# Local attention in units of two heads over 512 tokens, with the first expert products taken chunk by chunk between the units

## The chip, the cores and the metric

The kernel runs on one core of a Trainium2 chip. The engines named here are PE (TensorE, matrix products and transposes), ACT (ScalarE), DVE (VectorE), POOL (GpSimd) and SP (SyncE, whose queue issues the loads and stores). The metric is the device time of one launch in microseconds (us). The kernel before takes 873.11 us, the median of 3 runs (872.82 to 873.40).

## What is computed

Three steps follow each other, in float32 data with float64 weights for the two expert layers:

```python
# attention: 4 batches, 8 heads, 512 local and 32 global queries, head size 64
mask = np.abs(pos[:, None] - pos[None, :]) <= 32
s_l = concat([scale * q_l @ k_g.T, where(mask, scale * q_l @ k_l.T, -1e9)])
out_l = softmax(s_l) @ concat([v_g, v_l])
out_g = softmax(scale * q_g @ k_all.T) @ v_all
x = concat([out_g, out_l], axis=2)            # 2304 tokens x 512
# first expert layer: 512 -> 2048 -> 512
h = x @ w_in
y = elu(h) @ w_out
# second expert layer: 512 -> 1536 -> 512
xn = y / rms(y) * rms_g
out = (silu(xn @ w_gate) * (xn @ w_val)) @ w_o2
```

## The kernel before, in words

**Blocks.** The 2048 local tokens are four blocks of 512 (a batch each). A block needs its attention output `x` (four tiles of 128 tokens), its transpose `xT` (four chunks `c` of 128 features, each as a high and a low half in a reduced float type, since every large product is done in the three passes of `PASSES`, line 29), and then for each of 16 slices `j` of the hidden layer an *h product* (`mm1`, L127: 12 matmuls, three for each chunk) and a *y product* (`mm2`, L151: 12 matmuls, summed over all `j` in four PSUM tiles). Between them stands the activation (`act1` with `elu_a`, L137 and L120): on ACT a relu and an exp, on DVE a maximum, on ACT the high half of `g`, on DVE its low half.

**Attention units.** There are 16 local units `u`, four for each block. Each has five steps: S (`a_S`, 64 small matmuls), E (`a_E`: eight masked maxima on DVE, each followed by an exp on ACT), T (`a_T`: eight transposes on PE and two copies ET on ACT), PV (`a_PV`, 64 small matmuls) and N (`a_N`: the division, on DVE). S takes the load `kq`, PV the load `v`. Before the change, unit `u` is one tile of 128 tokens with all eight heads, so that each chunk of `xT` needs all four units of its block. Units 0 to 3 form the front; units 4 to 7 run inside block 0 for block 1, and so on.

**Weights.** They come as float64 words and are turned into two float32 halves, a pair of 128x512 tiles at a time: `abs` on ACT (L86), a shift (L93) and an or (L94) on DVE, the high half on ACT (`hi`, L97), the low half on DVE (`lo`, L100). Block 0 needs 16 such pairs, numbered 0 to 15 in `order1`: of each four, two are for `w_in` and feed four h products, and two are for `w_out` and feed two y products each. Pairs 0 to 2 are turned in the front, the others during block 0 (`w1_decode`, L394).

**Order.** PE always follows the written order. In the front (the `with` that starts behind L415) ACT and DVE follow it too; inside the blocks the builder's scheduler orders them, held by `issue_after`. Block 0 runs through `moe_block` (L324): for each `j` an h product, then the y product of `j - 1`, with the unit's steps between by `att_slot` (L299). The last lines of the block transpose `x` of the next block (`a_X`, L286) and subtract the low halves. The queue on SP is a single row: a load whose buffer is still in use holds all loads behind it.

**Idle products.** At the start PE does `NIDLE` = 61 matmuls of 64x64 zeros (L358) while the first load is on its way.

Of the kernel before, what the change touches and what calls it, by code (L numbers as in the profile page):

```python
# [21 lines left out]
P = 128  # L22
# [7 lines left out]
NIDLE = 61  # L30
# [11 lines left out]
def fused_kernel(ctx: ExitStack, tc: tile.TileContext, kq, vl, gkq, gv, w_in, w_out, w_gate, w_val, w_o2, rms_g, consts, out):  # L42
# [47 lines left out]

    def dec_bits(x, raw):
        word = words(raw)
        nc.vector.tensor_scalar(out=i32(x), in0=i32(x), scalar1=3, scalar2=None, op0=ALU.logical_shift_left)  # L93
        nc.vector.scalar_tensor_tensor(out=i32(x), in0=word[:, :, 0], scalar=29, in1=i32(x), op0=ALU.logical_shift_right, op1=ALU.bitwise_or)  # L94
# [32 lines left out]
    def mm1(xT, j, n):  # L127
        h = hps.tile([P, 512], F32, tag="h", name="h")
        G, o = j // 4, (j % 4) * P
        k = 0  # L130
        for c in range(4):
            for ws, xs in PASSES:
                nc.tensor.matmul(h[:, :n], W1[c, G][:, ws, o:o + P], xT[c][:, xs, :n], start=(k == 0), stop=(k == 11))  # L133
                k += 1
        return h

    def act1(h, n, fn=None):  # L137
# [4 lines left out]
        return g  # L142

# [51 lines left out]
    with ExitStack() as ls:  # L195
# [5 lines left out]
        zero = ac.tile([P, 64], BF16, name="zero")  # L201
# [15 lines left out]
        def load_v(u):  # L217
            if u < 16:
# [4 lines left out]
                t = t[:, :2080].rearrange("p (i h d) -> p i h d", i=4, h=8)  # L223
                nc.sync.dma_start(out=t, in_=vl[u].rearrange("p (i h d) -> p i h d", i=4, h=8))
                v_t[u] = t

        def a_S(u, pools):
            T = u % 4
            m = 0 if T == 0 else (2 if T == 3 else 1)
            t = kq_t.pop(u)  # L230
            ss = [pools[i][0].tile([P, 4, P], F32, tag=pools[i][1], name="s") for i in range(2)]
            for pr in range(4):
                for i in range(4):
                    for par in range(2):
                        r = slice(64 * par, 64 * par + 64)
                        nc.tensor.matmul(ss[par][32 * i:32 * i + 32, pr, :], t[r, pr, 224 + 32 * i:256 + 32 * i], t[r, pr, 32 * i:32 * i + 128],  # L236
                                         start=True, stop=True)
            s_t[u] = ss

        def a_E(u):  # L240
# [3 lines left out]
            T = u % 4  # L244
            mk_u = mask32[:, 0 if T == 0 else (2 if T == 3 else 1), :]
            for par in range(2):
                for pr in range(4):
                    nc.vector.tensor_tensor_reduce(out=e[par][:, pr, :], in0=ss[par][:, pr, :], in1=mk_u, scale=-SCALE, scalar=3.0e38,  # L248
                                                   op0=ALU.add, op1=ALU.min, accum_out=mx[:, par, pr:pr + 1])
                    nc.scalar.activation(e[par][:, pr, :], e[par][:, pr, :], AF.Exp, bias=mx[:, par, pr:pr + 1], scale=-1.0)  # L250
            e_t[u] = e

        def a_T(u, par, pool, tag):
            pt = pool.tile([P, 512], F32, tag=tag, name="ptp")
            for pr in range(4):
                nc.tensor.transpose(pt[:, pr * P:(pr + 1) * P], e_t[u][par][:, pr, :], ident)  # L256
# [16 lines left out]
        def a_N(u):  # L273
            b, T = u // 4, u % 4
            if T == 0:
                x_t[b] = moe.tile([P, 4, 512], F32, tag="x32", name="x")
            x = x_t[b][:, T, :].rearrange("p (a e d) -> p e a d", a=4, e=2)
# [1025 lines left out]
```

## Time and profile before

| | us |
|---|---|
| median of 3 runs | 873.11 |
| the profiled execution, its own time | 874.14 |
| its span, first to last instruction | 872.2 |
| PE busy in the span | 853.0 (98%) |
| DVE busy | 572.8 (66%) |
| ACT busy | 462.5 (53%) |

The trace counts microseconds from the start of the span. A row of the timeline gives the start, the length, the engine, the line, the operation with its tiles, the count, and in brackets the idle time before it and what ended that. "PEclk" is the clock that was granted to PE as a share of 2.4 GHz: 0.5 is the lower level, 1.2 GHz.

### The profile page before, as it was taken

To read this page: it belongs to the slowest core of one execution; us is meant where nothing else is said; L and a number is where in the kernel's file an instruction comes from. 1 tells how busy PE (TensorE), PEld (TensorE's weight loads), DVE (VectorE), ACT (ScalarE), POOL (GpSimd) and SP (SyncE) were. 2 spreads that over 40 slices of the span, in tenths; PEclk is the share of its full clock that TensorE was granted. 3 is DMA by queue.
4 is the path that set the end of the run, shared out by engine and by line. 5 is a ranking of instruction groups with operands and counts; after the bars stand their busy time and mean duration, and the time that the engine had idled before them with its cause. 6 is when DMAs were issued, how large, how long until landed. Compare 5 with 4: busy or idle time off the path is not lost.

```text
span 872.2 us, 16347 instructions
## 1 busy us (share of the span) xinstructions
PE 853.0 (98%) x6703; PEld 713.8 (82%) x6703; DVE 572.8 (66%) x1119; ACT 462.5 (53%) x788; POOL 8.0 (1%) x10
## 2 busy tenths in 40 slices
PE   7789999999999999999999999999999999999998
PEld 5567788888888888777878888878999888888998
DVE  3899637656575565544378788897987655555663
ACT  4789545555564455433273677764555444443442
POOL 0000000000000000000030000000000000000000
PEclk8899999999999999999999999999999999999999
DMA  9896525765578766442500687879523232329102
GB/s 355 327 381 232 196 84 204 260 240 204 210 280 281 235 211 218 163 168 94 171 26 25 219 292 240 260 246 340 248 75 119 73 97 73 98 72 397 62 25 86
DMA packets 92126, 165.49 MB, mean 190 GB/s; under 512 B 4884, under 2 KB 59284, under 8 KB 86932
## 3 DMA queue, kind: packets, MB, share of 16 engines
q1 hardware_dynamic: 92052, 164.45, 54.1%
q8 instruction: 53, 0.87, 0.4%
q14 instruction: 21, 0.17, 0.1%
HBM read 128.26 MB, written 36.18 MB: 189 GB/s over the span
## 4 chain that ended last, share of the span: by engine, by line
PE 88%; DVE 4%; DMA 3%; ACT 3%; issue 1%; SPq 0%; DVEq 0%; ACTq 0%
PE y L154 19%; PE h L133 18%; PE A L799 14%; PE c L1148 14%; PE Q L799 11%; PE pg L813 2%; DMA kq<-in_kq 2%; PE s L236 1%; PE yg L729 1%; PE hg L713 1%; PE o L269 1%; PE ptp L256 1%; PE og L833 1%; DVE dx L94 1%; DVE wA L100 1%
## 5 line engine op out<-in xcount | busy, mean ns | idle before, releaser
L154 PE MATMUL y<-g,wA 128*128 128x512 f32 x768 | 198.0, 401 | 4.4 <-DVE g L141 3.7
L133 PE MATMUL h<-xT,wA 128*128 128x512 f32 x768 | 186.6, 392 | 1.0 <-DVE xT L294 1.0
L154 PEld LDWEIGHTS y<-g,wA 128*128 128x128 f32 x768 | 140.5, 189 | 40.2 <-issue 5.7
L133 PEld LDWEIGHTS h<-xT,wA 128*128 128x128 f32 x768 | 143.7, 188 | 32.0 <-DVE xT L294 1.2
L799 PE MATMUL A<-xc,wS 128*128 128x512 f32 x576 | 138.9, 392 | 0.1
L799 PEld LDWEIGHTS A<-xc,wS 128*128 128x128 f32 x576 | 107.1, 188 | 23.1 <-DVE pp L852 0.8
L1148 PE MATMUL c<-wH,p 128*128 128x256 f32 x1008 | 125.3, 284 | 0.0
L1148 PEld LDWEIGHTS c<-wH,p 128*128 128x128 f32 x1008 | 123.0, 192 | 0.2
L799 PE MATMUL Q<-xc,wS 128*128 128x512 f32 x432 | 104.4, 391 | 0.7 <-DVE t L843 0.7
L799 PEld LDWEIGHTS Q<-xc,wS 128*128 128x128 f32 x432 | 80.2, 188 | 17.5 <-DVE t L843 1.2
L843 DVE TENSOR_TENSOR t<-t,Q 128x512 f32<-128x512 f32 x72 | 48.9, 684 | 49.2 <-ACT t L846 34.1
L838 ACT CAST p<-pp 128x512 fp32r<-128x512 f32 x84 | 51.3, 620 | 55.7 <-PE c L1148 51.1
L122 ACT ACTIVATE e<-h 128x512 f32<-128x512 f32 x48 | 28.8, 601 | 95.0 <-PE h L133 94.9
L846 ACT COPY t<-A 128x512 f32<-128x512 f32 x72 | 41.9, 585 | 62.3 <-PE A L799 62.1
L839 DVE TENSOR_TENSOR p<-pp,p 128x512 fp32r<-128x512 f32 x84 | 56.7, 686 | 21.6 <-ACT p L838 21.6
L124 DVE SCALAR_TENSOR_TENSOR e<-e,h 128x512 f32<-128x512 f32 x48 | 32.8, 683 | 54.6 <-ACT e L123 54.4
L604 DVE TENSOR_TENSOR wS<-wraw,wS 128x1024 fp32r<-128x1024 f32 x42 | 51.2, 1218 | 14.8 <-ACT wS L603 13.2
L140 ACT CAST g<-e 128x512 fp32r<-128x512 f32 x64 | 39.7, 620 | 35.6 <-DVE e L124 22.1
L141 DVE TENSOR_TENSOR g<-e,g 128x512 fp32r<-128x512 f32 x64 | 44.1, 689 | 19.2 <-ACT g L140 18.7
L603 ACT CAST wS<-wraw 128x1024 fp32r<-128x1024 f32 x42 | 43.9, 1045 | 1.7 <-DMA wraw<-wS 1.7
L250 ACT ACTIVATE E<-E,mx 128x128 f32<-128x128 f32 x128 | 39.7, 390 | 8.5 <-DVE mx L248 8.5
L849 ACT ACTIVATE t<-t 128x512 f32<-128x512 f32 x36 | 22.8, 632 | 39.0 <-DVE t L843 39.0
(197 smaller groups left out, 907.6 us busy)
## 6 DMA issues: line engine op xcount, KB each, us to landing
wH<-wH SPq DMA_DIRECT2D x20, 1024.0 KB, 9.2
wraw<-wS SPq DMA_DIRECT2D x36, 512.0 KB, 4.1
raw<-in_moe_w_out SPq DMA_DIRECT2D x14, 1024.0 KB, 5.6
raw<-in_moe_w_in SPq DMA_DIRECT2D x8, 1024.0 KB, 8.0
raw<-in_moe_w_gate SPq DMA_DIRECT2D x6, 1024.0 KB, 6.8
raw<-in_moe_w_val SPq DMA_DIRECT2D x6, 1024.0 KB, 5.5
wS<-raw SPq DMA_DIRECT2D x24, 256.0 KB, 2.2
gvr<-in_gv SPq DMA_DIRECT2D x8, 640.0 KB, 4.4
```

The costliest lines, as they stand in the source:

```text
L133: nc.tensor.matmul(h[:, :n], W1[c, G][:, ws, o:o + P], xT[c][:, xs, :n], start=(k == 0), stop=(k == 11))
L140: hi = nc.scalar.copy(g[:, 0, :n], e[:, :n])
L141: mark[:] = hi, nc.vector.tensor_tensor(out=g[:, 1, :n], in0=e[:, :n], in1=f(g[:, 0, :n]), op=ALU.subtract)
L154: nc.tensor.matmul(ys[dc][:, :n], W2[j][:, ws, dc * P:(dc + 1) * P], g[:, gs, :n], start=(j == 0 and k == 0), stop=(j == 15 and k == 2))
L603: nc.scalar.copy(t[:, :, 0, :], raw)
L604: nc.vector.tensor_tensor(out=t[:, :, 1, :], in0=raw, in1=f(t[:, :, 0, :]), op=ALU.subtract)
L799: nc.tensor.matmul(ps, w[:, 2 * (q % 4) + c, ws, :], x[:, c, xs, :], start=(first and c == 0 and z == 0), stop=(c == 1 and z == 2), skip_g ...
L838: hi = nc.scalar.copy(p[:, 0, :], src)
L839: mark[:] = hi, nc.vector.tensor_tensor(out=p[:, 1, :], in0=src, in1=f(p[:, 0, :]), op=ALU.subtract)
L843: mark[1] = nc.vector.tensor_tensor(out=t, in0=t, in1=ps, op=ALU.add)
L846: mark[0] = nc.scalar.copy(t, ps)
L1148: nc.tensor.matmul(ch[t // 2][:, 256 * (t % 2):256 * (t % 2) + 256], p[:, pl, t * P:(t + 1) * P], w[:, wl, :], start=(n in (0, 1, 3) and i ...
```

## The change

**Units.** Unit `u` of a block is now a pair of heads (one chunk `c` = u mod 4 of the features) over all 512 tokens of the block. The loads `kq` and `v` are laid out anew by the host for that; the counts and shapes of the matmuls, masks, exps and transposes of a unit stay as they were.

**Front.** Since unit `c` fills chunk `c` of `x` for the whole block, it can be transposed at once (`x_turn`, `x_hi`, `x_lo`), and the three matmuls of that chunk can be done for the h products of j = 0 and j = 1 (`mm1` with a range of chunks) before the next unit is done.

**Block 0.** Its first part (j = 0 to 3) is written out with ACT and DVE in written order; the rest is a loop of four `j` at a time in which each y product stands one h product later than before, and pairs are turned behind the marks of the activation before.

**Loads and idle products.** The first weight pair is loaded ahead of unit 0's `v`, the second ahead of unit 1's `v`, and the loads of unit 4 and of pairs 4 and 5 are written ahead of the front. `NIDLE` is 155, with matmuls of 32x32 on four column groups in turn.

```diff
-NIDLE = 61
+NIDLE = 155
-    def mm1(xT, j, n):
-        h = hps.tile([P, 512], F32, tag="h", name="h")
+    def mm1(xT, j, n, h=None, cs=range(4)):
+        if h is None:
+            h = hps.tile([P, 512], F32, tag="h", name="h")
...
-        for c in range(4):
-            for ws, xs in PASSES:
-                nc.tensor.matmul(h[:, :n], W1[c, G][:, ws, o:o + P], xT[c][:, xs, :n], start=(k == 0), stop=(k == 11))
-                k += 1
+        for c in cs:
+            for k, (ws, xs) in enumerate(PASSES):
+                nc.tensor.matmul(h[:, :n], W1[c, G][:, ws, o:o + P], xT[c][:, xs, :n], start=(c == 0 and k == 0), stop=(c == 3 and k == 2))
...
-            x = x_t[b][:, T, :].rearrange("p (a e d) -> p e a d", a=4, e=2)
+            x = x_t[b][:, :, c * P:(c + 1) * P].rearrange("p t (e d) -> p e t d", e=2)
...
+        def x_turn(b, c, pool, tag):
+            pt = pool.tile([P, 512], F32, tag=tag, name="xtp")
+            for T in range(4):
+                nc.tensor.transpose(pt[:, T * P:(T + 1) * P], x_t[b][:, T, c * P:(c + 1) * P], ident)
+            return pt
...
-            nc.tensor.matmul(idle[:64, :64], zero, zero, start=True, stop=True)
+        for k in range(NIDLE):
+            g = 32 * (k % 4)
+            nc.tensor.matmul(idle[g:g + 32, :32], zero, zero, start=True, stop=True)
...
+        w1_load()
         load_v(0)
         load_kq(1)
         w1_load()
         load_v(1)
         load_kq(2)
-        w1_load()
         load_v(2)
...
             a_S(0, ATT2)
             a_E(0)
...
+            a_PV(1, Y2)
             a_S(2, ATT2)
+            w1_shift(1)
+            a_N(1)
+            h01 = [mm1(xT, j, 512, None, (0,)) for j in range(2)]
+            x1 = x_turn(0, 1, yps, "y2")
+            x_hi(xT, 1, x1)
             a_E(2)
+            w1_or(1)
+            x_lo(xT, 1, x1)
...
+            for j in range(2):
+                mm1(xT, j, 512, h01[j], (3,))
+            e0 = act_exp(h01[0])
             w1_bits(2)
+            a_S(4, ATT2)
+            act_max(e0, h01[0])
             w1_hi(2)
+            h2 = mm1(xT, 2, 512)
...
+        def block0_act(j, h):
+            held_back = tuple(mark)
+            g = act1(h, 512, elu_a)
+            with behind(held_back):
+                w1_decode()
...
-        moe_block(0, slot0)
+        for j0 in range(4, 16, 4):
+            u, g = j0 // 4 + 4, {}
+            g[0] = block0_act(j0, mm1(xT, j0, 512))
+            mm2(ys, g3, j0 - 1, 512)
+            a_S(u, ATT2)
+            a_E(u)
+            load_kq(u + 1)
+            g[1] = block0_act(j0 + 1, mm1(xT, j0 + 1, 512))
+            h = mm1(xT, j0 + 2, 512)
+            a_T(u, 0, aps, "att")
+            a_T(u, 1, aps, "att")
+            mm2(ys, g[0], j0, 512)
+            g[2] = block0_act(j0 + 2, h)
+            a_PV(u, ATT2)
+            a_N(u)
+            load_v(u + 1)
+            h = mm1(xT, j0 + 3, 512)
+            g[3] = block0_act(j0 + 3, h)
+            if j0 == 12:
+                xT_t = {1: new_xT()}
+                a_X(1, (0, 1), xT_t[1], ATT2)
+            mm2(ys, g[1], j0 + 1, 512)
+            if j0 == 12:
+                a_X(1, (2, 3), xT_t[1], ATT2)
+            mm2(ys, g[2], j0 + 2, 512)
+            g3 = g[3]
```

PE, from unit 3's S in the front to the second h product; `s` is S, `ptp` is T, `o` is PV, `xtp` are the transposes of `x`. Before:

```order
L236 MATMUL s<-kq_185 32x128 x32
L269 MATMUL o<-v_183,ET 32x65 x32
L256 MATMUL ptp<-ident,E 128x128 x8
L269 MATMUL o<-v_187,ET 32x65 x32
L292 MATMUL xtp<-ident,x 128x128 x16
L133 MATMUL h<-xT_646,wA 128x512 x3
L133 MATMUL h<-xT_647,wA 128x512 x3
L133 MATMUL h<-xT_648,wA 128x512 x3
L133 MATMUL h<-xT_649,wA 128x512 x3
L236 MATMUL s<-kq__688 32x128 x32
```

The same place of the change:

```order
L256 MATMUL s<-kq_279 32x128 x32
L286 MATMUL o<-v_277,ET 32x65 x32
L139 MATMUL h<-xT_299,wA 128x512 x6
L274 MATMUL ptp<-ident,E 128x128 x8
L306 MATMUL xtp<-ident,x 128x128 x4
L286 MATMUL o<-v_281,ET 32x65 x32
L139 MATMUL h<-xT_300,wA 128x512 x6
```

The sixteen transposes of `x`, one piece before, are now four at a time, one chunk each, and the six matmuls of a chunk for both h products stand among the units.

ACT, at the start of block 0, from the first relu of a block's `h` on; `dx<-raw` is `abs`, `wA<-dx` is `hi`, `E` are a unit's exps. Before:

```order
L122 ACTIVATE e_706<-h_693 128x512
L97 CAST wA_680<-dx_603 128x2x512
L123 ACTIVATE e_706<-e_706 128x512
L97 CAST wA_776<-dx_772 128x2x512
L86 ACTIVATE dx_827<-raw_193 128x1024
L140 CAST g_710<-e_706 128x512
L250 ACTIVATE E_748<-E_748,mx_747 128x128 x4
L250 ACTIVATE E_749<-E_749,mx_747 128x128 x3
L122 ACTIVATE e_794<-h_781 128x512
L250 ACTIVATE E_749<-E_749,mx_747 128x128
L86 ACTIVATE dx_912<-raw_684 128x1024
L123 ACTIVATE e_794<-e_794 128x512
```

The same place of the change:

```order
L151 ACTIVATE e_807<-h_572 128x512
L152 ACTIVATE e_807<-e_807 128x512
L103 CAST wA_847<-dx_799 128x2x512
L160 CAST g_862<-e_807 128x512
L151 ACTIVATE e_866<-h_576 128x512
L152 ACTIVATE e_866<-e_866 128x512
L160 CAST g_886<-e_866 128x512
L86 ACTIVATE dx_889<-raw_285 128x1024
L268 ACTIVATE E_896<-E_896,mx_895 128x128 x4
L268 ACTIVATE E_897<-E_897,mx_895 128x128 x4
L151 ACTIVATE e_929<-h_849 128x512
L152 ACTIVATE e_929<-e_929 128x512
```

Before, the high halves of two pairs and the `abs` of a third stand between the first relu and the second; now one high half does, and both activations are through before the next `abs`.

DVE, at the end of block 0, at unit 7's N (`st` and `x`) ahead of the first low half of block 1's `xT`; `dx` are the shift and the or of a pair for the second layer. Before:

```order
L282 TENSOR_SCALAR st_1713<-o_1679 128x4
L283 RECIPROCAL st_1713<-st_1713 128x4
L284 TENSOR_TENSOR x_890<-o_1679,st_1713 128x4x64
L124 SCALAR_TENSOR_TENSOR e_1672<-e_1672,h_1659 128x512
L282 TENSOR_SCALAR st_1713<-o_1680 128x4
L283 RECIPROCAL st_1713<-st_1713 128x4
L284 TENSOR_TENSOR x_890<-o_1680,st_1713 128x4x64
L141 TENSOR_TENSOR g_1676<-e_1672,g_1676 128x512
L93 TENSOR_SCALAR dx_1734<-dx_1734 128x1024
L94 SCALAR_TENSOR_TENSOR dx_1734<-raw_1604,dx_1734 128x1024
L294 TENSOR_TENSOR xT0_1760<-xtp_1764,xT0_1760 128x512
```

The same place of the change:

```order
L299 TENSOR_SCALAR st_1813<-o_1779 128x4
L300 RECIPROCAL st_1813<-st_1813 128x4
L146 TENSOR_TENSOR g_1770<-e_1766,g_1770 128x512
L301 TENSOR_TENSOR x_1023<-o_1779,st_1813 128x4x64
L299 TENSOR_SCALAR st_1813<-o_1780 128x4
L92 TENSOR_SCALAR dx_1773<-dx_1773 128x1024
L300 RECIPROCAL st_1813<-st_1813 128x4
L95 SCALAR_TENSOR_TENSOR dx_1773<-raw_1631,dx_1773 128x1024
L301 TENSOR_TENSOR x_1023<-o_1780,st_1813 128x4x64
```

The second half of N's division stood ahead of the pair's shift and or, and now stands behind them.

## Rows read from the trace of the kernel before

**Rows 1.** The page, part 1: busy us (share of the span) and instructions.

```profile
PE 853.0 (98%) x6703; PEld 713.8 (82%) x6703; DVE 572.8 (66%) x1119; ACT 462.5 (53%) x788; POOL 8.0 (1%) x10
```

**Rows 2.** Windows, three stretches: length, then busy us by engine, PEclk, DMA share, GB/s.

```profile
5.07:38.09 33.02, 23.96 (x560) 17.34 (x560) 20.77 (x98) 21.37 (x50) 0.00 (x0) 0.84 1.01 406
38.09:93.47 55.38, 51.01 (x452) 40.07 (x453) 53.02 (x99) 46.15 (x70) 0.00 (x0) 0.97 0.80 292
93.47:145.86 52.39, 52.39 (x481) 42.76 (x480) 25.98 (x72) 26.82 (x53) 0.00 (x0) 1.00 0.38 129
```

**Rows 3.** Timeline of PE in the front: start, length, what, count, idle before.

```profile
0.95 3.46 PE L358 MATMUL idle<-zero 128*64 128x64 bf16 x61 [0.95 <-DVE cst L355]
5.07 1.46 PE L236 MATMUL s<-kq 64*32 64x128 f32 x64 [0.66 <-DMA kq<-in_kq]
...
12.35 1.85 PE L236 MATMUL s<-kq 64*32 64x128 f32 x64 [2.62 <-DMA kq<-in_kq]
14.13 1.96 PE L269 MATMUL o<-v,ET 128*32 128x65 f32 x64
...
25.68 1.16 PE L236 MATMUL s<-kq 64*32 64x128 f32 x64 [1.43 <-DMA kq<-in_kq]
```

**Rows 4.** Unit 3's v: its issue (timeline, SP) and its us to landing.

```profile
10.64 0.33 SPq L224 DMA_DIRECT2D v<-in_vl  x1
...
v<-in_vl SPq DMA_DIRECT2D x1, 1040.0 KB, 17.5
```

**Rows 5.** Timeline of PE in block 0 and at block 1's first h product.

```profile
38.09 3.00 PE L133 MATMUL h<-xT,wA 128*128 128x512 f32 x12 [0.96 <-DVE xT L294]
...
48.60 1.43 PE L154 MATMUL y<-g,wA 128*128 128x512 f32 x5 [2.37 <-DVE g L141]
...
51.19 2.71 PE L154 MATMUL y<-g,wA 128*128 128x512 f32 x6
...
57.62 3.03 PE L154 MATMUL y<-g,wA 128*128 128x512 f32 x12
...
93.47 2.88 PE L133 MATMUL h<-xT,wA 128*128 128x512 f32 x12
...
145.86 1.52 PE L133 MATMUL h<-xT,wA 128*128 128x512 f32 x6
```

**Rows 6.** Windows again, for the granted clock (the number behind POOL's).

```profile
12.35:16.00 3.65, 3.65 (x128) 3.11 (x128) 1.65 (x15) 1.20 (x2) 0.00 (x0) 0.53 1.01 425
...
50.00:53.30 3.30, 3.30 (x14) 2.92 (x13) 3.24 (x4) 3.30 (x7) 0.00 (x0) 0.52 1.02 415
53.30:93.50 40.20, 38.83 (x347) 30.62 (x347) 38.77 (x69) 33.62 (x48) 0.00 (x0) 1.00 0.80 288
```

**Rows 7.** Timeline of DVE: unit 0's N, then three instructions in direct succession.

```profile
16.04 0.16 DVE L282 TENSOR_SCALAR st<-o 128x4 f32<-128x4 f32 x1
...
17.53 0.68 DVE L93 TENSOR_SCALAR dx<-dx 128x1024 int32<-128x1024 int32 x1
...
75.11 0.69 DVE L141 TENSOR_TENSOR g<-e,g 128x512 fp32r<-128x512 f32 x1
75.71 1.22 DVE L100 TENSOR_TENSOR wA<-dx,wA 128x1024 fp32r<-128x1024 f32 x1
76.85 1.22 DVE L94 SCALAR_TENSOR_TENSOR dx<-raw,dx 128x1024 int32<-128x1024 int32 x1
```

**Rows 8.** Timeline of ACT, four entries in direct succession in block 0.

```profile
43.09 1.04 ACT L97 CAST wA<-dx 128x1024 fp32r<-128x1024 f32 x1
44.03 1.14 ACT L86 ACTIVATE dx<-raw 128x1024 f32<-128x1024 f32 x1
45.08 0.60 ACT L140 CAST g<-e 128x512 fp32r<-128x512 f32 x1
45.58 2.15 ACT L250 ACTIVATE E<-E,mx 128x128 f32<-128x128 f32 x7
```

More of the change, by code (lines that the diff above doesn't have):

```diff
@@ L142, in act1, with act_exp, act_max, act_hi @@
         return g
+    def act_exp(h):
+        e = moe.tile([P, 512], F32, tag="e", name="e", bufs=2)
+        nc.scalar.activation(e, h, AF.Relu, scale=-1.0)
+        nc.scalar.activation(e, e, AF.Exp, scale=-1.0)
+        return e
+    def act_max(e, h):
+        nc.vector.scalar_tensor_tensor(out=e, in0=e, scalar=-1.0, in1=h, op0=ALU.add, op1=ALU.max)
+    def act_hi(e):
+        g = moe.tile([P, 2, 512], F32R, tag="g", name="g", bufs=2)
+        mark[:] = nc.scalar.copy(g[:, 0, :], e), None
+        return g
+    def act_lo(g, e):
+        mark[1] = nc.vector.tensor_tensor(out=g[:, 1, :], in0=e, in1=f(g[:, 0, :]), op=ALU.subtract)
     mark = []
@@ L200, in fused_kernel @@
         mask32 = ac.tile([P, 3, P], F32, name="mask32")
-        zero = ac.tile([P, 64], BF16, name="zero")
+        zero = ac.tile([P, 32], BF16, name="zero")
         kq_t, v_t, s_t, e_t, et_t, o_t, x_t = {}, {}, {}, {}, {}, {}, {}
@@ L414, in fused_kernel, with turn_e @@
         w1_load(3)
+        load_kq(4)
+        load_v(4)
+        nc.sync.dma_start(out=gcol, in_=rms_g.rearrange("(c p) -> p c", p=P))
+        w1_load(2)
+        xT = new_xT()
+        def turn_e(u):
+            a_T(u, 0, yps, "y0")
+            a_T(u, 1, yps, "y1")
         with tc.manual_schedule(engines={mybir.EngineType.DVE, mybir.EngineType.Activation}):
@@ L447, in fused_kernel @@
-            a_PV(3, Y2)
-            a_N(3)
-            xT_t = {0: new_xT()}
-            a_X(0, (0, 1), xT_t[0], ATT2[:2] + HB)
-            last = a_X(0, (2, 3), xT_t[0], ATT2[:2] + HB)
+            turn_e(3)
+            x2 = x_turn(0, 2, aps, "att")
+            a_PV(3, Y2)
+            x_hi(xT, 2, x2)
+            x_lo(xT, 2, x2)
+            a_N(3)
+            for j in range(2):
+                mm1(xT, j, 512, h01[j], (2,))
+            x3 = x_turn(0, 3, aps, "att")
+            x_hi(xT, 3, x3)
@@ L452, in fused_kernel @@
+            x_lo(xT, 3, x3)
+            w1_abs(2)
+            for j in range(2):
+                mm1(xT, j, 512, h01[j], (3,))
+            e0 = act_exp(h01[0])
             w1_bits(2)
+            a_S(4, ATT2)
+            act_max(e0, h01[0])
             w1_hi(2)
+            h2 = mm1(xT, 2, 512)
+            g0 = act_hi(e0)
+            act_lo(g0, e0)
             w1_lo(2)
-        w1_load(2)
-        load_kq(4)
-        load_v(4)
-        nc.sync.dma_start(out=gcol, in_=rms_g.rearrange("(c p) -> p c", p=P))
+            e1 = act_exp(h01[1])
@@ new lines, in fused_kernel @@
+            act_max(e1, h01[1])
+            ys = new_y()
+            mm2(ys, g0, 0, 512)
+            g1 = act_hi(e1)
+            act_lo(g1, e1)
+            w1_abs(3)
+            w1_bits(3)
+            w1_load()
+            a_E(4)
+            load_kq(5)
+            h3 = mm1(xT, 3, 512)
+            e2 = act_exp(h2)
+            act_max(e2, h2)
+            w1_hi(3)
+            w1_abs(4)
+            w1_bits(4)
+            w1_lo(3)
+            w1_load()
+            g2 = act_hi(e2)
+            act_lo(g2, e2)
@@ new lines, in fused_kernel @@
+            a_T(4, 0, aps, "att")
+            a_T(4, 1, aps, "att")
+            mm2(ys, g1, 1, 512)
+            w1_hi(4)
+            w1_abs(5)
+            w1_bits(5)
+            w1_lo(4)
+            w1_load()
+            e3 = act_exp(h3)
+            act_max(e3, h3)
+            a_PV(4, ATT2)
+            w1_hi(5)
+            w1_lo(5)
+            w1_load()
+            a_N(4)
+            load_v(5)
+            mm2(ys, g2, 2, 512)
+            g3 = act_hi(e3)
+            act_lo(g3, e3)
```

142 lines of the change are left out of this document (69 added, 73 removed).

## The prediction

> **What bounds the kernel now.** PE is busy in 98% of the span [rows 1], so I looked first for the places where it is not. Three windows show them [rows 2]: in the front (5.07 to 38.09 us) PE is busy 23.96 of 33.02 us, in the first half of block 0 (to 93.47) 51.01 of 55.38, and from there to block 1's first h product 52.39 of 52.39. The change touches only what stands ahead of that product, so all it can win lies in 9.1 + 4.4 us of idle time and in what the lower clock costs: PEclk is 0.84 and 0.97 in the two stretches. Then I read the timeline of PE for what each wait ends on. In the front it is loads: S(1) waits 2.62 us and S(3) 1.43 us for `kq` [rows 3]. In block 0 it is the low half of `g` on DVE: 2.37 us ahead of the first y product [rows 5]. DVE is busy 53.02 of 55.38 us there and ACT 46.15 [rows 2]: with pairs of weights to turn, they are nearly as full as PE. So the question is whether ACT and DVE can deliver earlier, not whether PE can work earlier.
>
> **What the change leaves alone.** The matmuls, masks, exps, transposes and decodes are the same in number and shape; only idle products are added. I therefore add up dates: the longest chain through the new order, with durations from the rows, against 93.47 (the ninth h product, j = 8) and 145.86 (block 1's first h product) [rows 5]. Durations: on DVE a 128x512 instruction 0.69, a 128x1024 one 1.22, in direct succession 0.60 and 1.14 [rows 7]; on ACT `hi` 0.94, `abs` 1.05 (1.14 where the next waits for it), a 128x512 one 0.5 to 0.6, eight exps 8 x 0.307 = 2.45 [rows 8]; N 1.5 (16.04 to 17.53) [rows 7]; eight masks 1.8 (end of S(1), 14.2, to 16.04) [rows 3, 7]; an h or y product 2.75 and 3.0 behind small matmuls [rows 5]; S and PV 1.1 to 1.2 at the full clock, 1.85 and 1.96 at 0.53 [rows 3, 6]; a chunk's four transposes 0.6 with their tail, an estimate from these. The same addition over the order of before comes out within 0.3 us of 93.47.
>
> **Loads.** kq(1), with 2,704 KB loaded up to its end, lands at 12.3 [rows 3]; v(3), with 9,280 KB, at 10.64 + 17.5 = 28.1 [rows 4]: 2.40 us per 1,000 KB. The first weight pair ahead of v(0) makes that 3,024 KB, 13.1 us, and kq(1) 3,728 KB, 14.8, 2.5 later than before. From kq(3) on nothing moves.
>
> **The front.** PV(0) 13.1 to 15.0 at the lower clock, S(1) to 16.9, mask and eight exps to 19.7, xT chunk 0 high and ET to 20.8, PV(1) to 22.6, S(2) to 23.7, six h matmuls at 0.24 to 25.2, transposes of chunk 1 and its high half to 26.3 (ACT must do it ahead of E(2)), eight exps to 28.7, S(3) at the lower clock to 30.6, masks to 32.3, the low half of pair 1 to 33.4, N(2) to 34.9, chunk 2 turned, high, low to 36.7, N(3) to 38.2, chunk 3 and its high half to 39.4. Before, the first h product began at 38.09 [rows 5]. So the front is 1.3 us later, but two h products have only their last chunk left.
>
> **The head of block 0.** From 39.4: `abs`, shift, or of pair 2 to 42.4; `hi` 2 and `g` 0 high to 44.0; `g` 0 low, low 2, maximum 1 to 46.4; `g` 1 high, pair 3's three steps to 50.0; a mask and E(4)'s exps to 52.7; relu and exp of j = 2 to 53.9; `hi` 3, pair 4's three steps to 57.9; low 3 to 59.1; pair 5's three steps to 62.2; low 4, maximum 3, low 5 to 65.1; N(4) and `g` 3 low to 67.2; two shifts, maximum 4, two ors, `g` 4 low, low 6 to 73.1; `abs` 8, relu and exp 5, E(5)'s exps to 77.7; relu 6, `hi` 8, ET, exp 6, `g` 5 high, `abs` 9, ET to 82.4. Then PE alone: half a PV 0.53, h 7 2.75, y 5 3.0, y 6 2.75, to 91.4, where the ninth h product begins. Before it is 93.47: **2.1 us won**. PE itself could be further by then, with two h products all but done in the front; but the decodes of pairs 2 to 15 are not earlier, and in the written order ACT and DVE pass each step to each other. PE's waits would be about 1.4 us ahead of PV(4), 1.2 in y 2, 1.0 in y 3, 1.2 in PV(5).
>
> **The end of block 0.** From there PE has 52.4 us of work [rows 2]. Before, y 13 stood between PV(7) and h 15, so PE had 5.75 us from PV(7) to the transposes of block 1's chunk 0; now it has only h 15, 2.75 us. DVE's last `x` half stands behind the or of a pair. From S(7) on ACT and DVE need 0.3 + 2.45 (E) + 1.2 + 0.69 + 0.6 (j = 13) + 1.05 (`abs`) + 0.5 + 1.0 + 0.6 + 0.69 + 1.2 (ET, j = 14) + 0.4 + 0.2 + 0.6 + 1.14 + 0.4 = 13.0, some 0.5 of hand-overs and 0.7 since E(7) begins behind pair 15, j = 12: 14.2. PE needs 2.75 + 2.75 + 1.0 + 3.0 + 1.1 + 2.75 = 13.35. A **new wait** of 0.9 follows; its bounds are 0 (DVE in the order of before) and 2.2 (pair 15's load, behind v(7) on SP, some 1.5 late). The last low half of `xT` costs 0.4 more. 91.4 + 52.4 + 1.3 = 145.1, against 145.86: 0.7 us less, call it 0.6.
>
> **Idle products.** The trace has none of 32x32. Bounds: as long as one of 64x64, 3.46 / 61 = 57 ns, or as short as an S matmul, 1.16 / 64 = 18 ns [rows 3]: 155 end at 9.8 or at 3.8 us. I take the lower, since S also works on tiles of 32 columns; then the first load at 5.07 still decides. The Trainium skill (TensorE: Matmul & The Clock Gate, "Wait — 56ns, not 53.3ns?") states that small matmuls never start closer than about 25 ns; the trace disagrees with 18 ns for S. By that rule the 155 would end at about 4.8, an estimate from that page, ahead of the load all the same, which speaks against the overrun below.
>
> **The sum.** 874.14 of the profiled execution less 0.6 is 873.5; the median lies 1.03 lower, so **872.5**. A measurement of this kernel can tell about 0.2%, 1.75 us, from no change.
>
> **Rivals.** *The front at the full clock.* More matmuls stand in it, and before the clock was low in only a part of it, 0.84 on the mean [rows 2]. S(1) and S(3) then take 0.7 less each and PV(0) 0.2; with half of the new wait gone, 870.5. For: the six h matmuls of each chunk. Against: the load wait ahead of PV(0) is 3.4 us instead of 2.62. Chance 0.32. *The lower clock reaches the h products of the front.* If PE is found idle in T(1) (paced by exps) and the clock is low at 22 to 26 us, S(2) takes 0.7 more, the six matmuls twice 1.44, the transposes 0.3, and all of it stands ahead of E(2): 2.4 us, 874.9, slower. It decides from about 2.4 us on. Before, the clock was low in just such a stretch behind a wait, 12.35 to 16.00 [rows 6]. Chance 0.14. *Scattered waits bring the clock down in block 0.* After the 2.37 us wait the clock was 0.52 from 50.0 to 53.3, and six y matmuls took 2.71; after shorter waits, 53.3 to 93.5, it stayed 1.00 [rows 5, 6]. The new waits of 1.2 to 1.4 stand close together at 56 to 60; y 2 would take 2.75 more, of which 0.6 to 2 stays behind the decodes: 873.8. The Trainium skill ("TensorE: Matmul & The Clock Gate", "A second HAM failure mode: psum-queue depth-cycling") says that frequent short idles between groups of matmuls are enough to make the clock go up and down. By that rule y 2 would run at the lower level; this trace bears it out only for the one long wait, at 0.52 against 1.00. Chance 0.07. *The idle products overrun.* At 57 ns they hold S(0) back to 9.8, mask, exps, T and ET put PV(0) at 15.3 instead of 13.1: 874.7. Chance 0.05. That the change does nothing, since DVE sets the pace with the same 53 us of work, is the forecast's own neighbour: it wins 2.1 and loses most of it.
>
> **How the numbers follow.** Forecast 0.42. Faster by over 0.2% (below 871.36) is the first rival, 0.32; slower (above 874.86) is the second, half of the third and the fourth, 0.22; the rest, 0.46, is the same. The range reaches to the first rival with the whole new wait gone (872.5 - 1.6 - 0.9 = 870.0) and to the second with 0.6 of the third (875.5): 869.8 to 875.6.
>
> **What would show it.** Right: chunk 3's high half at about 39.4, PE waits for DVE and ACT between 50 and 83, the ninth h product near 91.4, none after it until a wait of about 1 us ahead of block 1's transposes on DVE `x`, block 1's first h product near 145.2. Wrong: no such waits in block 0 (then ACT and DVE were faster in succession than I added), PEclk of 0.5 between 22 and 26 us, or a first S later than 5.1.

## The result, and the profile after

The changed kernel takes 884.0 us (median of 4 runs, 883.26 to 884.81) against 873.25 us for the kernel before beside it: a ratio of 1.0123, 95% interval 1.0106 to 1.0141. It is slower by 10.8 us, where 872.5 was predicted and 875.6 was the upper end of the range. The profiled execution has a span of 881.6 us, 9.4 more than before.

First the same three stretches as in [rows 2], cut at the matching events: from the first score to the first product of chunk 3 (before: to the first h product), from there to the ninth h product, from there to block 1's first h product. A fourth line is a piece of the front. Ahead of them stand two lines of the page, on PE (busy us, share, instructions) and on a DMA queue (packets, MB, share of 16 engines). The columns of the stretches: length, busy us by engine, granted clock, share of the DMA engines, GB/s.

```profile
PE 855.2 (97%) x6797; PEld 713.2 (81%) x6797; DVE 573.9 (65%) x1119; ACT 462.5 (52%) x788; POOL 8.0 (1%) x10
...
q8 instruction: 53, 0.87, 0.4%
```

```profile
4.90:51.73 46.83, 32.72 (x578) 23.60 (x578) 20.80 (x98) 20.13 (x49) 0.00 (x0) 0.82 0.77 313
51.73:103.28 51.55, 46.75 (x435) 35.51 (x436) 43.70 (x89) 39.90 (x63) 0.00 (x0) 1.00 0.62 224
103.28:155.70 52.42, 52.42 (x482) 42.71 (x481) 37.68 (x85) 34.09 (x59) 0.00 (x0) 1.00 0.56 198
...
41.38:46.00 4.62, 4.62 (x49) 3.76 (x49) 1.53 (x6) 0.00 (x0) 0.00 (x0) 0.50 0.02 5
```

The ninth h product begins at 103.28 in place of 93.47 [rows 5], 9.8 later, and block 1's first at 155.70 in place of 145.86, 9.8 later too. The front takes 46.83 us in place of 33.02, 13.8 more. The stretch behind it takes 51.55 in place of 55.38, 3.8 less, and the last is as long as before. So the whole loss lies in the front. The timeline of PE there (start, length, line, operation, count, idle before it and what ended it):

```profile
0.94 1.46 PE L383 MATMUL idle<-zero 128*32 128x32 bf16 x155 [0.94 <-DVE cst L379]
4.90 1.96 PE L256 MATMUL s<-kq 64*32 64x128 f32 x64 [2.51 <-DMA kq<-in_kq]
7.74 2.53 PE L274 MATMUL ptp<-ident,E 128*128 128x128 f32 x8 [0.87 <-ACT E L268]
12.17 1.96 PE L286 MATMUL o<-v,ET 128*32 128x65 f32 x64 [1.90 <-DMA v<-in_vl]
14.06 1.94 PE L256 MATMUL s<-kq 64*32 64x128 f32 x58
18.05 0.42 PE L256 MATMUL s<-kq 64*32 64x128 f32 x6 [2.05 <-issue]
18.39 0.66 PE L306 MATMUL xtp<-ident,x 128*128 128x128 f32 x4
19.35 2.53 PE L274 MATMUL ptp<-ident,E 128*128 128x128 f32 x8 [0.30 <-ACT E L268]
22.64 1.96 PE L286 MATMUL o<-v,ET 128*32 128x65 f32 x64 [0.76 <-ACT ET L276]
24.53 1.52 PE L256 MATMUL s<-kq 64*32 64x128 f32 x45
28.46 0.62 PE L256 MATMUL s<-kq 64*32 64x128 f32 x19 [2.41 <-issue]
29.01 2.45 PE L139 MATMUL h<-xT,wA 128*128 128x512 f32 x6
31.26 1.06 PE L306 MATMUL xtp<-ident,x 128*128 128x128 f32 x4
33.29 2.37 PE L274 MATMUL ptp<-ident,E 128*128 128x128 f32 x8 [0.98 <-ACT E L268]
35.59 1.16 PE L256 MATMUL s<-kq 64*32 64x128 f32 x64
36.68 0.58 PE L286 MATMUL o<-v,ET 128*32 128x65 f32 x25
41.38 1.31 PE L286 MATMUL o<-v,ET 128*32 128x65 f32 x39 [4.12 <-issue]
42.62 2.92 PE L139 MATMUL h<-xT,wA 128*128 128x512 f32 x6
```

Three times PE stops in the middle of 64 equal products, whose operands have long been there: 2.05, 2.41 and 4.12 us, 8.58 in all. They are released by "issue": no semaphore explains them. No such row stands in the kernel before.

What ends them can be counted. A product is two instructions, a weight load and a matmul. From the first stop to the second there are 6 + 4 + 8 + 64 + 45 = 127 products, from the second to the third 19 + 6 + 4 + 8 + 64 + 25 = 126; with two and four recorded wait instructions that is 256 both times. And queue 8, of kind "instruction", carries 53 packets and 0.87 MB, 16.4 KB each, while PE has 2 x 6797 = 13,594 products' instructions: 256 per packet. So **queue 8 brings PE's program in pieces of 256 instructions, and PE stops at the end of a piece when the next is not there.** In the trace the packets start at 4.99, 15.86, 26.14 and 39.00 us, and PE goes on 2.2, 2.3 and 2.4 us after the last three. The view of the DMA queues has them when it is asked for a short window; from 15.85 to 15.87 us it says:

```profile
q8 instruction: 1, 0.02, 293.4%
```

The change and nine of the kernels below have 24 such stops in all, and behind each of them PE goes on 2.2 to 2.4 us after the start of a packet of queue 8. The Trainium skill (Runtime: NRT & Kernel Launch, "Instruction fetch mechanics") describes such blocks of 256 instructions and says that crossing into the next is mostly hidden. In the kernel before it is; here it costs 8.58 us.

The stops cost more than their length: behind the longest the granted clock is 0.50, the lower of its two levels, from 41.38 to 46.00, and it is 0.50 behind the first too, from 22 to 26 us. Over the front it is 0.82.

### The profile page after: what moved, and what is told of

Read it like the earlier page. It is cut to its first block, busy times and chain, and to the rows that moved or that the text cites. A ratio compares the mean times of both kernels' runs of the same rounds, so it can differ in the third digit from the quotient of the medians.

```text
span 881.6 us, 16537 instructions
## 1 busy us (share of the span) xinstructions
PE 855.2 (97%) x6797; PEld 713.2 (81%) x6797; DVE 573.9 (65%) x1119; ACT 462.5 (52%) x788; POOL 8.0 (1%) x10
## 4 chain that ended last, share of the span: by engine, by line
PE 89%; DVE 4%; ACT 4%; issue 2%; DMA 1%; SPq 0%; ACTq 0%; DVEq 0%
PE y L176 19%; PE h L139 18%; PE A L922 14%; PE c L1271 14%; PE Q L922 11%; PE pg L936 2%; PE o L286 2%; PE s L256 2%; PE ptp L274 1%; PE yg L852 1%; PE hg L836 1%; DMA v<-in_vl 1%; PE og L956 1%; ACT E L268 1%; DVE dx L95 1%
## 5 line engine op out<-in xcount | busy, mean ns | idle before, releaser
L176 PE MATMUL y<-g,wA 128*128 128x512 f32 x768 | 193.8, 397 | 1.8 <-DVE g L164 1.8
L139 PE MATMUL h<-xT,wA 128*128 128x512 f32 x768 | 190.8, 397 | 1.8 <-ACT xT L310 0.7
L128 ACT ACTIVATE e<-h 128x512 f32<-128x512 f32 x44 | 26.1, 594 | 79.8 <-PE h L139 79.8
L130 DVE SCALAR_TENSOR_TENSOR e<-e,h 128x512 f32<-128x512 f32 x44 | 30.1, 684 | 46.2 <-ACT e L129 46.1
L145 ACT CAST g<-e 128x512 fp32r<-128x512 f32 x60 | 37.3, 621 | 38.2 <-DVE e L130 23.3
L146 DVE TENSOR_TENSOR g<-e,g 128x512 fp32r<-128x512 f32 x60 | 41.3, 689 | 20.3 <-ACT g L145 19.9
```

The source lines that it names most:

```text
L146: mark[:] = hi, nc.vector.tensor_tensor(out=g[:, 1, :n], in0=e[:, :n], in1=f(g[:, 0, :n]), op=ALU.subtract)
L176: nc.tensor.matmul(ys[dc][:, :n], W2[j][:, ws, dc * P:(dc + 1) * P], g[:, gs, :n], start=(j == 0 and k == 0), stop=(j == 15 and k == 2))
```

## The experiments

A kernel's name begins with a_ where it is the changed kernel with an edit, with b_ where it is the kernel before with one.

**The count of idle products.** Idle products move the ends of the pieces along the work and leave the order of the work and of the loads as it is. Theory A is the late piece; its rivals are the new order or its loads (B) and the clock (C). The edit, here for 61; 27, 91, 123, 171 and 187 differ in this number alone:

```diff
-NIDLE = 155
+NIDLE = 61
```

> The changed kernel with 61 of its small idle products in place of 155; nothing else differs. Theory A (PE's program arrives in pieces of 16384 bytes, 256 instructions, over queue 8; in the changed kernel PE stands before instructions 705, 961 and 1217 of its stream because the next piece is late, 2.05 + 2.41 + 4.12 us): 188 instructions fewer ahead move the three places by 94 products, to the 26th product of unit 1's scores, the 12th of unit 2's scores and the 57th of unit 3's scores; stalls with issue as releaser stand there and nowhere else, and the time is 873 to 884. Rival B (the new order of the front itself, or its loads, costs the 10 us): the stalls stay at the products where they were, or the time stays at 884 within 1 us whatever the stalls do. Rival C (the idle products keep the clock up): the scores of unit 0 and 1 run at the low clock, time above 884.

> The changed kernel with 27 idle products. The boundaries fall to unit 0's transposes (8.5 us), the 60th product of unit 1's scores (16), the 47th of unit 2's scores (22.5) and the 28th of unit 2's PV (29.5), one fewer before 38 us than with 155. By the ways between them (7.5, 6.5 and 7 us against 3 to 4 us of the piece and 2.2 us until it can be used) no stall: 870.4 within 1.5. If a boundary in unit 0's transposes is what makes the next piece late, as with 155, stalls of 2 to 4 us before 449 or 705: 873 to 884.

> The changed kernel with 91 idle products, so that the first boundary of PE's program pieces (instruction 193) falls behind the idle products, at the 5th product of unit 0's scores, and the others at the end of unit 0's PV, the 47th product of unit 1's PV, the 28th of unit 3's scores and the 8th of unit 3's PV. Theory A1 (a piece comes 3 to 4 us after its boundary and can be used 2.2 us later; only where the way to the next boundary is shorter than that, some 6 us, does PE stand, and a late piece makes the next ones late): no stall, 870.4 within 1.5. Theory A2 (every boundary more in the loaded stretch costs, so the time grows evenly with the count of idle products, 0.14 us a product from 61 to 155): 874.5.

> The changed kernel with 123 idle products: instruction 193 falls among the idle products, 449 to the 28th product of unit 0's PV (about 13 us), 705 to the 15th of unit 1's PV (about 21 us), 961 to unit 3's transposes' neighbourhood (about 27 us), 1217 to the end of unit 2's PV. Theory A1: every way between two boundaries is 6.5 us or longer, no stall, 870.4 within 1.5. Theory A2 (even growth): 879. Theory A3 (what hurts is that the piece boundary 193 is passed during the idle products, before the data are there): stalls as with 155, 882 to 885.

> The changed kernel with 187 idle products: 193 falls among them, 449 to the 36th product of unit 0's scores (about 6 us, 1 us after the piece before it came), 705 to the 28th product of unit 1's scores, 961 to the 14th of unit 2's scores, 1217 to the 59th of unit 3's scores. Theory A1: 9, 8 and 7 us between boundaries, so no stall, 870 to 872. Theory A2 or A3: 884 to 889, with stalls before 705, 961 and 1217.

| idle products | time, us | ratio to before, 95% interval | stops by issue in the profile, us |
|---|---|---|---|
| 27 | 883.53 | 1.0108 to 1.0138 | 2.61, 4.14, 2.85 |
| 61 | 870.42 | 0.9957 to 0.9980 | none |
| 91 | 871.81 | 0.9970 to 0.9989 | none |
| 123 | 877.57 | 1.0028 to 1.0061 | 3.81 |
| 155 (the change) | 884.0 | 1.0106 to 1.0141 | 2.05, 2.41, 4.12 |
| 171 | 881.42 | 1.0076 to 1.0114 | 0.38, 2.41, 3.04 |
| 187 | 874.89 | 1.0009 to 1.0028 | 0.76, 3.18 |

The time neither grows with the count nor falls with it. 27 and 155 differ by 128 products, that is one piece, and give the same time, with stops at the same products. The timeline of PE with 27:

```profile
13.90 1.68 PE L256 MATMUL s<-kq 64*32 64x128 f32 x58
18.18 0.42 PE L256 MATMUL s<-kq 64*32 64x128 f32 x6 [2.61 <-issue]
...
23.82 0.91 PE L256 MATMUL s<-kq 64*32 64x128 f32 x45
28.87 1.06 PE L256 MATMUL s<-kq 64*32 64x128 f32 x19 [4.14 <-issue]
...
38.35 0.91 PE L286 MATMUL o<-v,ET 128*32 128x65 f32 x25
42.11 1.02 PE L286 MATMUL o<-v,ET 128*32 128x65 f32 x39 [2.85 <-issue]
```

58, 45 and 25 products, as with 155. I had expected 870.4 of this kernel, or stops where a piece ends in unit 0's transposes; it is the second. With 61 there is no stop. That is not what theory A had expected, stops at the moved places and 873 to 884 us, and B and C did not come true either. The trace shows why none came: the ends of pieces lie 6.2 to 9.2 us apart in this kernel and the packets start 3.2 to 3.6 us after them, so each piece is there in time. Its timeline, then its three stretches:

```profile
0.94 0.67 PE L383 MATMUL idle<-zero 128*32 128x32 bf16 x61 [0.94 <-DVE cst L379]
4.87 1.96 PE L256 MATMUL s<-kq 64*32 64x128 f32 x64 [3.26 <-DMA kq<-in_kq]
...
12.40 1.96 PE L286 MATMUL o<-v,ET 128*32 128x65 f32 x64 [2.17 <-DMA v<-in_vl]
14.29 1.96 PE L256 MATMUL s<-kq 64*32 64x128 f32 x64
...
21.53 1.16 PE L256 MATMUL s<-kq 64*32 64x128 f32 x64
22.61 1.68 PE L139 MATMUL h<-xT,wA 128*128 128x512 f32 x6
```

```profile
4.87:38.71 33.84, 26.99 (x579) 19.35 (x579) 20.44 (x98) 20.17 (x49) 0.00 (x0) 1.00 1.01 410
38.71:90.27 51.56, 46.75 (x435) 35.50 (x435) 43.69 (x89) 39.90 (x63) 0.00 (x0) 1.00 0.66 240
90.27:142.65 52.38, 52.38 (x482) 42.71 (x480) 37.72 (x85) 34.19 (x59) 0.00 (x0) 1.00 0.56 197
```

Chunk 3 is reached 13.0 us earlier than in the changed kernel (38.71 against 51.73): PE is idle there for 6.9 us in place of 14.1 and busy for 27.0 in place of 32.7, since the products that followed a stop ran at the lower clock (the six h products of chunk 0 take 1.68 us in place of 2.45). The two later stretches have the same length to 0.05 us. This kernel beats both. With 91 there is no stop either, and the time is within what A1 expected; unit 1's PV and unit 2's scores take 1.96 and 1.82 us in place of 1.11 and 1.16, which is the 1.4 us more.

The expectations on 123 and 187 failed under every theory: 123 has a stop before the 58th product of unit 2's PV, 187 two. With 123 only 3.3 us lie between two ends of pieces, at 26.2 and 29.5, where A1 had counted on 6.5, and the packet came at 31.19. A2's even growth came near with 123 alone (879 against 877.57).

**Fewer instructions for the same idle time, and the order of the loads.**

```diff
-NIDLE = 155
+NIDLE = 7
 ...
-            nc.tensor.matmul(idle[g:g + 32, :32], zero, zero, start=True, stop=True)
+            nc.tensor.matmul(idle, zero[:, :P], zero, start=True, stop=True)
```

> The changed kernel with 7 idle products of 512 columns in place of 155 of 32: about as long on PE, 296 instructions fewer. Theory A: the boundaries move 148 products later in the work (449 to the 4th product of unit 1's PV, 705 into the first h products, 961 to the 48th product of unit 2's PV), so one boundary less falls in the loaded stretch up to 40 us, and its stalls go down to at most two: 873 to 881. Rival B (order or loads): 884 within 1.5. Rival C (clock): the idle work is as long as before, so no change of the clock in the first 14 us.

881.36 us (ratio 1.0080 to 1.0114), two stops, 1.77 and 2.80 us, behind the first of the h products and behind the 45th product of unit 2's PV. Theory A had at most two, and a time up to 881. The stops are 4.57 us in place of 8.58, 4.0 less, and the profiled execution is shorter by about as much, 879.27 against 883.39. The medians differ by 2.6 only; the other executions of this kernel, 881.23 to 882.19, were not seen in a trace.

```diff
-        w1_load()
         load_v(0)
         load_kq(1)
         w1_load()
         load_v(1)
         load_kq(2)
+        w1_load()
```

> The changed kernel with the first ten loads in the order of the kernel before (v(0) and kq(1) ahead of the first weight pair, the second pair after kq(2)); the rest is unchanged. Theory A with a late piece because of the order of the loads ahead of it: the pieces come about 3 us after their boundaries, as in the kernel before, the three stalls go, and the time is 873 to 877. Theory A where the load order does not matter: the stalls stay at the same three products, 2 to 4 us each, 882 to 886. Rival B (work order): 884 within 1.5 without a change of the stalls.

883.48 us (1.0101 to 1.0132): the same three products, 2.48, 2.51 and 2.92 us. So the load order is not the cause of the stops. One thing moved: unit 0's PV began at 10.31 in place of 12.17, and the piece for instruction 705 came at 13.44 in place of 15.86.

**Other idle counts in the kernel before.**

```diff
-NIDLE = 61
+NIDLE = 155
 ...
-            nc.tensor.matmul(idle[:64, :64], zero, zero, start=True, stop=True)
+            g = 32 * (k % 4)
+            nc.tensor.matmul(idle[g:g + 32, :32], zero, zero, start=True, stop=True)
```

> The kernel before with 155 idle products of 32x32 in place of its 61 of 64x64. Theory A (late pieces of PE's program): the piece boundaries, which lie in the kernel before at instructions 705, 961 and 1217, move 94 products earlier in the work; PE's idle time gets rows released by issue at the 60th product of unit 0's PV, the 51st of unit 1's PV and the 42nd of unit 2's PV if the piece takes as long as in the changed kernel (7 to 10 us after the boundary before), and the time rises to 876 to 882; if a piece still comes 3 us after its boundary, as it does in the kernel before, there is no stall and the time is 873 within 1.5. Rival B (the order of the front): 873 within 1.5, no stalls.

> The kernel before with 187 idle products of 32x32 (188 instructions and 64 more than b_idle155 has): the boundary 449 falls to the 36th product of unit 0's scores, 1 us after the piece before it came. Theory A (position of the boundaries, not the new order): a stall of 0.5 to 1 us at that product as in a_idle187 and a piece that is late afterwards, a second stall of up to 3 us before 705 at the 27th product of unit 0's PV; 873.5 to 878. Rival B (only the new order can be caught by the boundaries): no stall, 873 within 1.

With 155: 875.65 us, ratio 1.0017 to 1.0040, runs from 872.55 to 877.79. The profiled one is the fastest and has no stop, so the 2.5 us of the others were not seen in a trace. With 187: 871.56, ratio 0.9973 to 1.0014, no difference, with runs from 870.21 to 879.71; the slowest has no trace. The profile has the short stop that theory A expected, behind the 36th product of unit 0's scores, but neither the second stop nor the longer time:

```profile
4.75 1.49 PE L236 MATMUL s<-kq 64*32 64x128 f32 x36 [2.09 <-DMA kq<-in_kq]
6.90 1.10 PE L236 MATMUL s<-kq 64*32 64x128 f32 x28 [0.66 <-issue]
```

So the order of before can be caught as well, but in these two kernels it lost much less.

**Is it the load on the DMA engines?** Two tries to hold the later loads back failed: in a_defer they were moved in the program but issued from 11.95 us on, much as in the changed kernel (12.05), and in a_hold only weight pair 2 was held (to 36.10), while the loads written behind it were issued ahead of it. The single row on SP is thus a row in the order of issue, which here was not the written one. The DMA engines stayed full (shares of 0.93 to 1.03 up to 40 us). The edits (shortened):

```diff
 a_defer:
+            with tc.issue_after(held.ins):
+                w1_load(3)
 ...
 a_hold:
+            nc.scalar.copy(f(words(hold2)[:, 0:1, 0]), xT[1][:, 0, 0:1].bitcast(F32))
+            nc.sync.dma_start(out=hold2, in_=w_src(*order1[2]))
```

> The changed kernel (155 idle products) with the loads behind v(3) (weight pairs 2 to 6, kq(4), v(4), the gains) held until the high half of xT's chunk 1 is written, so that the DMA engines run dry at about 24 us and stay so until that copy. Theory A (a piece is late because it stands behind data on busy DMA engines): the stall before 705 stays (2 us, at 16 us), the piece for 961, asked for at 18 us, comes about 1 us after the engines run dry or sooner and its stall shrinks or goes, the one before 1217 (4.1 us) goes if its piece is asked for before the held loads start; time 878 to 882 as far as the held loads bring no new wait. Rival (the boundaries cost by themselves, loaded or not): the three stalls stay, 884 or more.

> The changed kernel (155 idle products) with a one-column copy by ACT, behind unit 2's exponentials and turns, into the buffer of weight pair 2, which that pair's load must wait for; the loads of weight pairs 2 to 6, kq(4), v(4) and the gains stand behind it. So the DMA engines run dry at about 25 us and stay so to about 35 us, which the move of the loads in a_defer did not bring about. Theory A (a piece of PE's program is late because of the data on the DMA engines): the stall before 705 at 16 us stays; the piece whose packet came at 26.1 us comes at 24 to 26, and the piece asked for at 28 us comes 1 us later, so the stall of 4.1 us before 1217 goes and the one before 961 shrinks: 877 to 881. Rival (late by itself, whatever is on the DMA engines): three stalls as in the changed kernel, 884 or more.

884.33 (1.0107 to 1.0141) and 881.11 us (1.0077 to 1.0107), with stops before the same three products each: 2.33, 2.41, 3.52 and 2.32, 2.41, 2.88. They say nothing on the load; they show that the stops are not the chance of a single execution. The third try put the front behind its loads:

```diff
-NIDLE = 155
+NIDLE = 153
 ...
+        late = v_t[4][:, 0, 0, 0, 0:32]
+        nc.tensor.matmul(idle[:32, :32], late, late, start=True, stop=True)
```

> The changed kernel with its idle products (one product that reads v(4), two instruction pairs, and 153 of the others: the same count of instructions as 155) held until v(4) is in, so that the whole front runs some 35 us later, after nearly all of its loads, at the same boundaries of PE's program pieces. It leaves nothing out; its time holds the 35 us of waiting and is not to be compared, the front's own length is. Theory A (a piece is late because of the data on the DMA engines): every piece comes about 1.1 us after its boundary, no stall released by issue at the 58th product of unit 1's scores, the 45th of unit 2's scores and the 25th of unit 2's PV, and from the first score to chunk 3's high half 34 us or less in place of 46. Rival (the request itself goes out late at these boundaries, whatever the DMA engines do): the stalls stay, 1 to 3 us each, and the pieces come more than 4 us after their boundaries.

```profile
37.53 1.96 PE L256 MATMUL s<-kq 64*32 64x128 f32 x64
40.37 2.38 PE L274 MATMUL ptp<-ident,E 128*128 128x128 f32 x8 [0.88 <-ACT E L268]
42.89 1.96 PE L286 MATMUL o<-v,ET 128*32 128x65 f32 x64
44.78 1.79 PE L256 MATMUL s<-kq 64*32 64x128 f32 x64
...
72.17 0.50 PE L139 MATMUL h<-xT,wA 128*128 128x512 f32 x1 [0.68 <-ACT xT L310]
```

Two stretches of it, in the columns of the windows above:

```profile
46.50:51.20 4.70, 3.20 (x20) 1.70 (x12) 4.14 (x23) 3.99 (x11) 0.00 (x0) 0.84 0.69 227
51.20:60.00 8.80, 7.03 (x141) 5.49 (x141) 6.29 (x26) 3.70 (x9) 0.00 (x0) 0.70 0.01 3
```

No stop, at the same ends of pieces. From the first score to chunk 3 it is 72.17 - 37.53 = 34.6 us, against 46.8 in the changed kernel. Its time, 905.22 us, holds the waiting for the loads and says nothing. While the DMA engines are idle (share 0.01 from 51.20 on) a packet starts 0.6 to 0.8 us after the end of a piece (55.59 after 54.97, 63.66 after 62.90), but 4.9 us after it (51.00 after 46.10) while two weight pairs are loaded. **Without the load on the DMA engines the stops are gone.** One thing more is gone with it: unit 0's PV no longer waits 1.90 us for `v`. Load and wait were not separated, since the two tries that kept the waits failed. One piece is telling: the end in unit 0's transposes is passed between 41.25 and 41.54, and the packet starts at 43.59, over 2 us later though the DMA engines are idle there (share 0.02), and 0.70 us after unit 0's PV began.

**When is a piece asked for?** In the stalled runs the late packets start not a fixed time after the end of a piece but 2.8 to 3.9 us after the start of the next large group behind a wait: 15.86 after PV(0) at 12.17, 26.14 after PV(1) at 22.64, 39.00 after unit 3's scores at 35.59, and 13.44 after 10.31 in a_loads. In the kernel before, where the ends of pieces lie within such groups, it is 3.0 to 3.6 us after the end. 171 idle products put an end of a piece ahead of unit 0's transposes, long before PV(0):

> The changed kernel with 171 idle products: the boundary 449 falls to the 53rd product of unit 0's scores (about 6.6 us), with 40 instructions between it and PE's wait ahead of unit 0's PV; 705 to the 42nd of unit 1's scores, 961 to the 29th of unit 2's scores, 1217 to the 9th of unit 2's PV. Theory A with a constant way of 3 us: the piece comes at 9.7 us, no stall there, 870.4 to 873. Theory P (in the stalled runs each piece's packet comes 3.1 to 3.8 us after PE gets past the next wait into a dense group, PV(0), PV(1) or S(3), not after the boundary): packet at 15.5 to 16 us, a stall of about 2.5 us before the 42nd product of unit 1's scores, then two more; 880 to 884.

```profile
12.08 1.96 PE L286 MATMUL o<-v,ET 128*32 128x65 f32 x64 [0.87 <-DMA v<-in_vl]
13.97 1.51 PE L256 MATMUL s<-kq 64*32 64x128 f32 x42
17.90 0.63 PE L256 MATMUL s<-kq 64*32 64x128 f32 x22 [2.41 <-issue]
...
22.70 1.96 PE L286 MATMUL o<-v,ET 128*32 128x65 f32 x64 [0.76 <-ACT ET L276]
24.60 1.09 PE L256 MATMUL s<-kq 64*32 64x128 f32 x29
28.73 1.14 PE L256 MATMUL s<-kq 64*32 64x128 f32 x35 [3.04 <-issue]
```

The packets came at 15.65 and 26.50, 3.57 after PV(0) and 3.80 after PV(1), and the stops stand at the 42nd and 29th products: theory P, though the third of its stops stayed away and one of 0.38 us stood before the 53rd product of unit 0's scores. It looks as if a late piece is asked for only when PE gets past its next wait, and then takes some 3.5 us on loaded DMA engines. That is not shown, since no trace holds the request itself, and three packets speak against it. In the changed kernel the first end of a piece falls among the idle products, at 1.69, and its packet starts at 4.99, only 0.09 us after the first group behind a wait. In a_unload the packet at 51.00 is ahead of unit 1's PV at 51.99. In b_idle155 the same end in unit 0's transposes is followed by a packet at 10.68, ahead of the next group at 11.83, where it is 13.44 in a_loads and 15.86 in the changed kernel. **What stays open** is therefore why these pieces came late; that they were late, and that PE stood until they came, is shown.

**The chunk-by-chunk sum alone.** With 61 idle products, both h products made whole behind the last chunk:

```diff
-            h01 = [mm1(xT, j, 512, None, (0,)) for j in range(2)]
 ...
-                mm1(xT, j, 512, h01[j], (3,))
+            h01 = [mm1(xT, j, 512) for j in range(2)]
```

> The changed kernel with 61 idle products and without its sum chunk by chunk: the first two h products are made whole, behind chunk 3's low half, so 18 of their 24 products (0.24 us each at full clock, 4.3 us) come after the last chunk. If the chunk-by-chunk sum is worth what the prediction gave it, the start of the exponential on h(0) comes some 2 us later and that on h(1) 4.3 us later than with a_idle61, and the time is 872.5 to 874.7. If DVE's and ACT's weight splits set the end of the front anyway, 870.4 within 1.

871.87 us (0.9978 to 0.9998), 1.45 more than with the sum in pieces: between the two forecasts, 872.5 to 874.7 and 870.4 within 1. The 24 products take 5.74 us from 38.80, and the scores behind them begin at 44.47 in place of 40.79. Of these 3.7 us 2.4 are given back up to the ninth h product (91.60 in place of 90.27); the wait of 1.02 us ahead of unit 4's PV, for one, is gone there.

## Why the prediction missed

- **The front** is the step that failed: chunk 3's high half was put at 39.4 and ended at 51.7. The dates were added up from loads, semaphores and durations; that PE's own program has to arrive was in none of the terms, and it cost three stops of 8.58 us and the lower clock behind them, which the prediction had named as a sign of being wrong (0.50 from 22 to 26 us). With the stops taken away by the idle count alone, the high half begins at 38.07 and ends near 38.7, so the dates themselves were 0.7 too late.
- **The idle products** failed twice. Their time was bounded by 18 and 57 ns and is 1.46 us / 155 = 9.4 ns, below both. The Trainium skill (TensorE: Matmul & The Clock Gate, "Wait — 56ns, not 53.3ns?") states some 25 ns as the least distance of two starts, however small the matmul; the 9.4 ns here differ, and the measurement decides. The wrong bound cost nothing, since the load decides (first score at 4.90, predicted 5.07). But they were priced as PE time alone; their 188 more instructions, which shift every end of a piece, were given no price, and moving those ends by 94 products was worth 13.6 of the 884 us (155 against 61).
- **The head of block 0** was right: 52.0 from the end of chunk 3's high half to the ninth h product, measured 51.6 in the changed kernel (51.7 to 103.28) and 51.6 with 61 (38.7 to 90.27). The waits stand where they were forecast, somewhat shorter, and the clock stays at 1.00: ahead of unit 4's PV 1.02 (forecast 1.4), in y 2 1.15 (1.2), in y 3 0.65 (1.0), in unit 5's PV 0.81 (1.2). With 61 idle products the first two are:

```profile
56.26 1.15 PE L286 MATMUL o<-v__197,ET 128*32 128x65 f32 x64 [1.02 <-ACT ET L276]
...
58.99 2.79 PE L176 MATMUL y<-g,wA 128*128 128x512 f32 x11 [1.15 <-DVE g L164]
```

- **The end of block 0**: the new wait of 0.9 and the 0.4 behind it did not come; 52.42 and 52.38 us, as before [rows 2]. The lower bound, 0, was right.
- **The rivals.** With 61 idle products the time is that of the front at the full clock, 870.5 predicted, 870.42 measured, with a recorded clock of 1.00 over the front. That the numbers meet is luck in part: the rival had its gain from faster scores and PV of units 0, 1 and 3 and half of the new wait, but unit 0's PV and unit 1's scores still took 1.96 us each. Against the forecast's own dates, block 1's first h product came 2.45 us early (142.65 against 145.1): 0.7 in the front, 0.4 in the head of block 0, 1.3 at its end. The lower clock did reach the h products of the front in the changed kernel (2.45 us at 29.01), as the second rival has it, but behind a stop: the same six take 1.68, 1.66 and 1.64 us with 61, 91 and 123 idle products, where no stop stands ahead of them. None of the slower rivals was the mechanism.

## What to carry to other kernels

Where long runs of small products stand beside a full load of the DMA engines, count instructions as well as time: a piece of 256 is used up in 2.3 us of them (two groups of 1.16 us), and the next may not be there. "issue" ahead of an engine in the middle of a group of equal instructions, at even distances in instructions, is the sign of it. Then shift the count of instructions ahead (here the idle products) before judging the order of the work, or a good order is thrown away for its position.

## What the runs showed of the hardware

- Idle products of 32x32 in bf16 that alternate between four groups of 32 columns start 9.4 ns apart (155 in 1.46 us), against 57 ns for 61 of 64x64 [rows 3].
- The packet with a later piece of PE's program started 0.6 to 0.8 us after the end of a piece with idle DMA engines (in a_unload; one there, at 43.59, came over 2 us after). With full ones it was 3.0 to 3.6 us in the kernel before and with 61 idle products, and up to 10.5 in the stalled runs (39.00 after 28.46). After each of the 24 stops PE went on 2.2 to 2.4 us after the start of a packet.
- The recorded clock does not tell all: with 61 idle products it is 1.00 from 12.40 to 16.25, and unit 0's PV and unit 1's scores take 1.96 us each, as long as at 0.53 in [rows 3, 6]. Why is open.

```profile
12.40:16.25 3.85, 3.85 (x129) 3.29 (x130) 2.77 (x8) 1.04 (x1) 0.00 (x0) 1.00 1.03 427
```
